# All of w_out loaded ahead of batch 1, whose q, k, v come by halves of heads and are worked off between the output products of chunk 0; kv masked in one op per pair

## Chip, cores, metric

One core of one Trainium2 chip. The metric is device time in microseconds (us) of one execution. The chip and the granted TensorE clock are named where they matter.

Engines: PE is TensorE (PEld its weight loads), ACT ScalarE, DVE VectorE, POOL GpSimd, SP the engine that issues most loads and stores.

## The reference

```python
# q, k, v: (8 batches, 8 heads, 576 rows, 64), float32
q_s = softmax(q, axis=-1)          # per row
k_s = softmax(k, axis=2)           # over the 576 rows
kv  = einsum('bhsd,bhse->bhde', k_s, v)
x   = einsum('bhsd,bhde->bhse', q_s, kv)      # -> (4608, 512)
h   = x @ w_in                     # (512, 2048)
g   = h * sigmoid(beta * h)
out = g @ w_out                    # (2048, 512)
```

## The kernel before

The rows are worked off in nine chunks of 512: chunks 0 to 6 are the first 512 rows of batches 0 to 6, chunk 7 the last 64 rows of all batches, chunk 8 the first 512 rows of batch 7. A chunk has 64 h products (16 units of four, each unit ending in one tanh on ScalarE and one product g on DVE) and 64 output products, all 128x128 by 512 columns. While chunk n runs, batch n+1's attention is prepared between its units ("hooks"). Batches 0 and 1 have nothing to hide behind: batch 0 is worked off at the start, batch 1 between chunk 0 and chunk 1.

```python
    def kv_half(b, half):                  # batches 2 to 7
        kv_mm(b, 2 * half)                 # both halves in bank K
        kv_mm(b, 2 * half + 1)
        kv_norm(b, 2 * half, 2)            # reciprocal, then two ops of 64 rows each

    def h_bank(n, i):
        if n == 0 and i < 12:
            return ("H0", "H1", "H2", "A0", "A1")[i % 5]
        ...
    # loads: q0, k0 (both halves), v0, w_in, w_out 0..11, then
    #        q1, k1, v1, w_out 12..15, q2, k2, v2      (13 buffers)
    ...
        if n == 0:
            b_mm(44)                       # 44 output products of chunk 0
            q_exp(1, 0, 4); q_exp(1, 4, 8) # (one per line in the kernel)
            ...                            # sums, divisions, k_exp
            q_t_pe(1, 0, nc.vector, "X0")
            b_mm(4)
            q_t_pe(1, 1, nc.vector, "H2")
            ...
            lead_in(1, ...)                # v casts, kv, x, with products on
                                           # zeros as fillers
```

The softmax here doesn't subtract the row's maximum and nothing guards it: scores larger than these inputs give would overflow.

Of the kernel before, what the change touches and what calls it, by code (L numbers as in the profile page):

```python
# [16 lines left out]
def kernel(  # L17
# [56 lines left out]
    w_out_b = const.tile([P, NJ, DM], BF16, name="w_out_b")  # L74
    kvp = [const.tile([P, HP, P], BF16, name=f"kvp{b}") for b in range(B)]
# [191 lines left out]
    def v_cast(b, h, eng):  # L267
        hf, a = divmod(h, 4)
        cast(
            eng,  # L270
            va[b % 2][:, 1:K5, h // 2, (h % 2) * D : (h % 2 + 1) * D],
            ld["v", b, hf][:, a, D:].rearrange("p (t d) -> p t d", t=K5 - 1),
        )
# [3 lines left out]
    def kv_mm(b, j, n="K"):  # L277
# [3 lines left out]
        for t in range(K5):  # L281
# [5 lines left out]
            )  # L287

# [21 lines left out]
    def kv_half(b, half):  # L310
        kv_mm(b, 2 * half)
        kv_mm(b, 2 * half + 1)
        kv_norm(b, 2 * half, 2)
# [43 lines left out]
    def h_bank(n, i):  # L357
        if n == 0 and i < 12:
            return ("H0", "H1", "H2", "A0", "A1")[i % 5]
        if n == 1 and i < 2:  # L360
            return ("X0", "H1")[i]
        return f"H{(n * NJ + i) % 3}"
# [26 lines left out]
    for n in range(NCH):  # L389
        if n == 0:  # L390
            bq += [(n, st, j) for j in range(12) for st in range(4)]
            bq += [(n, st, j) for st in (2, 3, 0, 1) for j in range(12, NJ)]
            continue
# [3 lines left out]
        for st in (2, 3):  # L397
# [5 lines left out]
    def b_mm(m):  # L403
        while m and pos[0] < len(bq):
# [3 lines left out]
            if j == 0:  # L408
                name = (f"A{st % 2}", ("A0", "A1", "X1", "K")[st])[n == 0]
                acc[n, st] = bank(name, [P, DM], F32, f"acc{n}_{st}")  # L410
            nc.tensor.matmul(  # L411
                acc[n, st][:],
                gs[n, j][:, st * P : (st + 1) * P],
                w_out_b[:, j, :],
# [8 lines left out]
    def store(n, st):  # L423
        o = osp.tile([P, DM], F32, tag="o", name=f"o{n}_{st}")
        if n == 0 and st % 2:
# [12 lines left out]

    nc.vector.memset(zero[:], 0.0)  # L439
    for hf in range(2):  # L440
        load_q(0, hf)
    for hf in range(2):
        load_kv("k", k, 0, hf, True)
    load_kv("v", v, 0, 0, True)
    load_kv("v", v, 0, 1, True, 0, 2)
    load_kv("v", v, 0, 1, True, 2, 4)
    nc.scalar.activation(beta_h[:, 0:1], zero[:, 0:1], ACTF.Exp)
    nc.scalar.dma_start(beta_r[:], moe_beta.rearrange("(j p) -> j p", p=P))
    load_w_in(0, 256)
# [4 lines left out]
    for j0 in range(0, 12, 2):  # L454
# [8 lines left out]
    nc.vector.tensor_reduce(even[:], evens[:], axis=AX.X, op=ALU.add)  # L463
    for i in range(2):
# [5 lines left out]
    for b in range(B):  # L470
# [11 lines left out]
    q_sum(0, 0, 4)  # L482
    q_sum(0, 4, 8)
    q_div(0, 0, NT, nc.gpsimd, 0, 4)
    q_div(0, 0, NT, nc.vector, 4, 8)
    k_exp(0, 0, 4)
    k_exp(0, 4, 8)
    q_t_pe(0, 0, nc.vector)
    dummy(3)
    q_t_pe(0, 1, nc.vector)  # L490
# [3 lines left out]
    dummy(4)  # L494



    def lead_in(b, kb, xb, fill):
        v_first(b, 0)
        v_cast(b, 0, nc.gpsimd)  # L500
        v_cast(b, 1, nc.gpsimd)
        v_cast(b, 2, nc.scalar)
        v_cast(b, 3, nc.vector)
        fill(0)
        kv_mm(b, 0, kb[0])
        kv_mm(b, 1)
        v_first(b, 1, 0, 1)
        v_cast(b, 4, nc.gpsimd)
        v_cast(b, 5, nc.scalar)
        v_first(b, 1, 1, 2, nc.scalar)  # L510
        v_cast(b, 6, nc.gpsimd)
        v_cast(b, 7, nc.scalar)
        kv_mm(b, 2, kb[1])
        kv_norm(b, 0, 2)
        fill(1)
        x_mm(b, 0, xb[0])
        kv_mm(b, 3)
        x_mm(b, 1, xb[1])
        kv_norm(b, 2, 1)
        x_out(b, 0, nc.scalar)  # L520
        x_out(b, 1, nc.scalar)
        fill(2)
        x_mm(b, 2, xb[2])
        kv_norm(b, 3, 1)
        x_out(b, 2, nc.vector)
        if b == 0:
            cast_w_in(0, 0, nc.gpsimd, 0, 128)
            cast_w_in(0, 0, nc.gpsimd, 128, 256)
        fill(3)
        x_mm(b, 3, xb[3])  # L530
# [132 lines left out]
```

## Time and profile before

| | before |
|---|---|
| time | 294.63 us median (294.43 to 294.85, 4 runs) |
| span of the profiled run | 293.0 us |
| TensorE busy | 97% of the span |
| first h product that is followed without a break | 17.66 us |
| first output product of chunk 0 | 31.62 us |
| first h product of chunk 1 | 49.23 us, after 48 output products |
| last product to end of span | 3.9 us |

How to read a row of the following table of busy time by stretch: the stretch in us, its length, then busy us of PE, PEld, DVE, ACT, POOL (with instruction counts), the granted clock, the DMA share and GB/s.

```profile
0.00:16.40 16.40, 14.72 (x78) 6.52 (x79) 10.31 (x25) 8.75 (x12) 10.82 (x31) 1.00 0.92 306
...
31.60:42.60 11.00, 11.00 (x61) 5.31 (x60) 6.61 (x8) 5.79 (x7) 5.56 (x7) 1.00 1.05 344
42.60:49.20 6.60, 4.45 (x39) 2.32 (x37) 4.25 (x14) 2.51 (x6) 3.16 (x5) 1.00 0.99 329
49.20:80.00 30.80, 30.12 (x154) 14.15 (x154) 21.84 (x43) 21.81 (x38) 8.21 (x13) 1.00 0.80 248
80.00:110.00 30.00, 30.00 (x162) 14.19 (x160) 18.71 (x39) 19.32 (x34) 8.91 (x15) 1.00 0.75 188
...
289.00:293.00 4.00, 0.10 (x1) 0.00 (x0) 0.00 (x0) 0.60 (x1) 0.00 (x0) 1.00 0.17 66
```

From 49 us on TensorE looks full. What can be gained lies in the first 49 us and in the last 4. Each 512-column product is recorded with 0.38 us, while the next one starts 0.216 us later (the Trainium skill, "Trainium Kernel Development and Optimization", Performance Expectations: matmuls are pipelined).

TensorE's timeline around batch 1, and the place where batch 2's kv products wait (start, length, what; in brackets the idle time before it and what ended it):

```profile
41.12 0.61 PE L210 MATMUL tp<-ident,Eq 128*128 128x128 bf16 x8
...
44.31 1.01 PE L282 MATMUL kv<-va,Ek 128*128 128x130 bf16 x15 [0.63 <-DVE va L265]
45.16 0.59 PE L625 MATMUL spare<-zero 128*128 128x512 bf16 x2
...
48.05 0.39 PE L323 MATMUL x<-qT,kvp 128*128 128x512 bf16 x1 [1.02 <-DVE kvp L303]
...
49.23 1.89 PE L368 MATMUL h<-xT,w_in_b 128*128 128x512 bf16 x8 [0.35 <-DVE xT L158]
...
66.79 0.73 PE L282 MATMUL kv<-va,Ek 128*128 128x130 bf16 x10 [0.66 <-DVE kvp L303]
```

The reader is to see a chain of single steps from 41 to 49 us, with products on zeros ("spare") in its gaps, and one visible wait at 66.8 us.

The same later, in batch 4. Its second kv half starts 1.04 us after the four h products ahead of it, although four products take 0.863. No idle time is noted, because the 0.18 us lie under the recorded end of the last h product:

```profile
148.46 1.03 PE L368 MATMUL h<-xT,w_in_b 128*128 128x512 bf16 x4
149.32 0.73 PE L282 MATMUL kv<-va,Ek 128*128 128x130 bf16 x10
...
150.75 1.03 PE L368 MATMUL h<-xT,w_in_b 128*128 128x512 bf16 x4
151.79 0.39 PE L282 MATMUL kv<-va,Ek 128*128 128x130 bf16 x4
```

The end of the span: the last eviction takes 0.60 us and its store follows.

```profile
289.19 0.60 ACT L428 ACTIVATE o<-acc 128x512 f32<-128x512 f32 x1 [2.90 <-PE acc L411]
```

### The profile page before, as it was taken

The page shows a single profiled execution, that of the slowest core. Times are in us where ns is not written, and L with a number is a line of the kernel's source. Part 1 is how long each engine was busy: PE and PEld are TensorE (multiplying, and loading weights), DVE is VectorE, ACT ScalarE, POOL GpSimd, SP SyncE. Part 2 cuts the span into 40 slices and gives each one's busy share as a digit, 9 for nine tenths or more (in the row PEclk, how much of TensorE's full clock was granted, in tenths as well). Part 3 has the DMA queues.
Part 4 walks back from the last instruction along what each step waited for, and adds up shares of the span by engine and source line. Part 5 has one row for each costly group of instructions (what it writes and reads, how often), then busy time and mean ns, then how long its engine had stood idle before and what let it go on. Part 6 is the DMA issues. An engine that isn't in the chain of part 4 may idle for free.

```text
span 293.0 us, 4194 instructions
## 1 busy us (share of the span) xinstructions
PE 283.7 (97%) x1453; PEld 131.7 (45%) x1453; DVE 162.0 (55%) x309; ACT 168.9 (58%) x274; POOL 77.4 (26%) x131
## 2 busy tenths in 40 slices
PE   8999997999999999999999999999999999999994
PEld 3534443444445444544454445444544444444441
DVE  3867385966766466655665576547554433443300
ACT  4566473874884568456855685468544544354411
POOL 8476743450171027101720062106200000000000
PEclk9999999999999999999999999999999999999999
DMA  7999999879459935991399329911410110031111
GB/s 237 357 385 385 362 327 346 295 184 362 100 142 304 284 42 130 313 294 36 105 281 337 50 78 261 360 39 73 107 39 0 72 39 36 0 73 38 36 72 72
DMA packets 54966, 51.67 MB, mean 176 GB/s; under 512 B 21136, under 2 KB 46752, under 8 KB 54944
## 3 DMA queue, kind: packets, MB, share of 16 engines
q1 hardware_dynamic: 54912, 51.39, 58.7%
q8 instruction: 11, 0.18, 0.3%
q14 instruction: 11, 0.09, 0.1%
q10 hardware_dynamic: 32, 0.01, 0.0%
HBM read 38.28 MB, written 9.44 MB: 163 GB/s over the span
## 4 chain that ended last, share of the span: by engine, by line
PE 82%; DMA 14%; DVE 2%; issue 1%; ACT 0%; POOL 0%; SPq 0%; ACTq 0%; POOLq 0%
PE acc L411 39%; PE h L368 37%; DMA v<-in_v_dram 5%; DMA wo<-in_moe_w_out_dram 4%; DMA wi<-in_moe_w_in_dram 3%; PE kv L282 3%; PE x L323 2%; DMA q<-in_q_dram 2%; DVE kvp L303 1%; POOL va L153 0%; PE xt L338 0%; DVE xT L158 0%; ACT th L380 0%; DVE g L382 0%; DVE rk L293 0%
## 5 line engine op out<-in xcount | busy, mean ns | idle before, releaser
L382 DVE SCALAR_TENSOR_TENSOR g<-th,h 128x512 bf16<-128x512 bf16 x144 | 98.6, 686 | 102.5 <-ACT th L380 102.3
L380 ACT ACTIVATE th<-h,beta_h 128x512 bf16<-128x512 f32 x144 | 98.7, 687 | 94.7 <-PE h L368 94.0
L411 PE MATMUL acc<-w_out_b,g 128*128 128x512 bf16 x576 | 145.9, 379 | 0.0
L368 PE MATMUL h<-xT,w_in_b 128*128 128x512 bf16 x512 | 129.2, 379 | 1.2 <-DVE g L382 0.6
L368 PEld LDWEIGHTS <-w_in_b 128*128 128x128 bf16 x576 | 56.3, 98 | 69.5 <-issue 2.2
L411 PEld LDWEIGHTS <-g 128*128 128x128 bf16 x576 | 55.3, 98 | 63.9 <-issue 1.0
L193 POOL TENSOR_TENSOR Eq<-Eq,qz 128x512 bf16<-128x512 bf16 (+1 forms) x26 | 28.9, 1113 | 94.4 <-DVE qz L190 70.5
L428 ACT ACTIVATE o<-acc 128x512 f32<-128x512 f32 x34 | 20.2, 594 | 9.0 <-PE acc L411 9.0
L251 ACT ACTIVATE Ek<-k 128x640 bf16<-128x640 f32 (+1 forms) x28 | 22.6, 806 | 2.7 <-DMA k<-in_k_dram 2.7
L189 DVE TENSOR_REDUCE qz<-Eq 128x8 f32<-128x512 bf16 (+1 forms) x28 | 21.2, 756 | 5.1 <-ACT Eq L181 5.1
L181 ACT ACTIVATE Eq<-q 128x512 bf16<-128x512 f32 (+1 forms) x28 | 19.3, 690 | 6.4 <-DMA q<-in_q_dram 6.4
L153 POOL TENSOR_SCALAR_AFFINE_SELECT va<-v 128x256 bf16<-128x256 f32 x56 | 20.8, 407 | 5.2 <-DMA v<-in_v_dram 4.7
L368 PE MATMUL h<-xTt,w_in_b 128*128 128x512 bf16 x64 | 16.4, 379 | 0.0
L323 PE MATMUL x<-qT,kvp 128*128 128x512 bf16 x32 | 12.2, 381 | 1.6 <-DVE kvp L303 1.5
L282 PE MATMUL kv<-va,Ek 128*128 128x130 bf16 x160 | 11.9, 219 | 1.3 <-DVE kvp L303 0.7
L144 ACT CAST xT<-x 128x512 bf16<-128x512 f32 (+1 forms) x18 | 9.9, 557 | 5.7 <-PE x L323 5.7
L477 PE MATMUL warm<-zero 128*128 128x512 bf16 x37 | 11.8, 471 | 1.3 <-DVE zero L439 1.3
L282 PEld LDWEIGHTS <-Ek 128*128 128x128 bf16 x160 | 10.1, 97 | 6.5 <-issue 4.4
L158 DVE CAST xT<-x 128x512 bf16<-128x512 f32 (+1 forms) x16 | 10.4, 652 | 0.8 <-PE x L323 0.5
L303 DVE TENSOR_TENSOR kvp<-kv,rk 64x128 bf16<-64x128 f32 (+1 forms) x36 | 9.9, 274 | 0.9
L235 POOL TENSOR_TENSOR Et<-Et,zt 128x512 bf16<-128x512 bf16 x4 | 4.2, 1042 | 22.4 <-ACT th L380 11.4
L153 POOL TENSOR_SCALAR_AFFINE_SELECT w_in_b<-wi 128x1024 bf16<-128x1024 f32 (+1 forms) x9 | 8.5, 945 | 4.7 <-DMA wi<-in_moe_w_in_dram 4.7
(44 smaller groups left out, 73.5 us busy)
## 6 DMA issues: line engine op xcount, KB each, us to landing
k<-in_k_dram SPq DMA_DIRECT2D x28, 320.0 KB, 6.5
v<-in_v_dram SPq DMA_DIRECT2D x26, 320.0 KB, 7.6
q<-in_q_dram SPq DMA_DIRECT2D x16, 512.0 KB, 5.2
out_dram<-o SPq DMA_DIRECT2D x32, 256.0 KB, 2.5
wi<-in_moe_w_in_dram SPq DMA_DIRECT2D x8, 512.0 KB, 7.8
wo<-in_moe_w_out_dram SPq DMA_DIRECT2D x8, 512.0 KB, 12.2
k<-in_k_dram SPq DMA_DIRECT2D x4, 256.0 KB, 7.1
qt<-in_q_dram SPq DMA_DIRECT2D x8, 128.0 KB, 7.9
```

Source lines behind the costliest of these rows:

```text
L153: nc.gpsimd.affine_select(out=dst, in_=src, pattern=[[0, n]], base=0, channel_multiplier=0, compare_op=ALU.is_equal, fill=fill0,)
L181: nc.scalar.activation(Eq[b][:, :, h0:h1, :].rearrange("p t h d -> p h t d"), ld["q", b, hf][:, a : a + h1 - h0, :].rearrange("p h (t d) - ...
L189: nc.vector.tensor_reduce(qz[b][:, :, h], Eq[b][:, :, h, :], axis=AX.X, op=ALU.add)
L193: eng.tensor_tensor(Eq[b][:, t0:t1, h0:h1], Eq[b][:, t0:t1, h0:h1], qz[b][:, t0:t1, h0:h1].unsqueeze(3).to_broadcast((P, t1 - t0, h1 - h0, ...
L251: nc.scalar.activation(Ek[b][:, :, h0:h1, :].rearrange("p t h d -> p h t d"), ld["k", b, hf][:, a : a + h1 - h0, :].rearrange("p h (t d) - ...
L282: nc.tensor.matmul(kvs[b, j // 2][:, j % 2, :], Ek[b][:, t, 2 * j : 2 * j + 2, :].rearrange("p h d -> p (h d)"), va[b % 2][:, t, j, :], st ...
L323: nc.tensor.matmul(xps[b, j][:], kvp[b][:, j, :], qT[b][:, :, j, :], start=True, stop=True)
L368: nc.tensor.matmul(hs[n, i][:], w_in_b[:, kt, i * P : (i + 1) * P], rhs_a(n, kt), start=(kt == 0), stop=(kt == KT - 1),)
L380: nc.scalar.activation(th[:], h[:], ACTF.Tanh, scale=beta_h[:, i : i + 1])
L382: nc.vector.scalar_tensor_tensor(out=g[:], in0=th[:], scalar=1.0, in1=h[:], op0=ALU.add, op1=ALU.mult)
L411: nc.tensor.matmul(acc[n, st][:], gs[n, j][:, st * P : (st + 1) * P], w_out_b[:, j, :], start=(j == 0), stop=(j == NJ - 1),)
L428: nc.scalar.activation(o[:], acc[n, st][:], ACTF.Copy, scale=0.5)
```

## The change

Intent: fill TensorE with more of chunk 0's output products while batch 1 lands, and let batch 1's steps follow each other in smaller pieces with output products between them. The parts:

1. Load order: all eight w_out pieces ahead of batch 1; k and v by halves of heads (k half 0, v half 0, k half 1, v half 1); the first w_in piece in two.
2. Batches 0 and 1 are worked off per pair of heads in banks of their own, with one masked op per pair. The 64 output products of chunk 0 are dealt out: 32, exps of q1, 16, exp of k1, 9, then 2, 1, 1, 1 between batch 1's steps, two left for chunk 1.
3. Chunk 0's h products use five banks throughout; the hooks of chunk 1 move back by one or two units.
4. Batches 2 to 7: the second kv half goes to an X bank.
5. The last output tile is computed in two column halves, the second one evicted by two engines and stored in two pieces.

```diff
+    def kv_mask(b, j):
+        ...
+        nc.vector.scalar_tensor_tensor(
+            out=kvp[b][:, j, :], in0=kv1[b, j][:, 0 : 2 * D], scalar=rks[b, j][:, 0:1],
+            in1=mask[:], op0=ALU.mult, op1=ALU.mult,
+        )
     def kv_half(b, half):
-        kv_mm(b, 2 * half)
+        kv_mm(b, 2 * half, xbank() if half else "K")
     def h_bank(n, i):
-        if n == 0 and i < 12:
+        if n == 0:
             return ("H0", "H1", "H2", "A0", "A1")[i % 5]
+    def loads(b):
+        for hf in range(2):
+            load_q(b, hf)
+        load_kv("k", k, b, 0, True)
+        load_kv("v", v, b, 0, True)
+        load_kv("k", k, b, 1, True)
+        load_kv("v", v, b, 1, True, 0, 2)
+        load_kv("v", v, b, 1, True, 2, 4)
-    for j0 in range(0, 12, 2):
+    for j0 in range(0, NJ, 2):
         load_w_out(j0)
+    def batch_1():
+        b_mm(32)
+        q_exp(1, 0, 4)
+        q_exp(1, 4, 8)
+        q_sum(1, 0, 4)
+        q_div(1, 0, NT, nc.gpsimd, 0, 4)
+        b_mm(16)
+        k_exp(1, 0, 4)
+        q_sum(1, 4, 8)
+        q_div(1, 0, NT, nc.vector, 4, 8)
+        b_mm(9)
+        q_t_pe(1, 0, nc.vector, "X0")
+        for h in range(4):
+            v_cast(1, h, nc.scalar if h % 2 else nc.gpsimd, 0)
+        kv_pair(1, 0, "X1")
+        kv_pair(1, 1, "K")
+        kv_mask(1, 0)
+        kv_mask(1, 1)
+        q_t_pe(1, 1, nc.vector, "H2")
+        ...
+        b_mm(2)
+        x_mm(1, 0, "X0")
+        b_mm(1)
+        x_mm(1, 1, "H2")
+        ... (heads 4 to 7 in the same way, then nine h products of chunk 1)
```

More of the change, by code (lines that the diff above doesn't have):

```diff
@@ L74 @@
     w_out_b = const.tile([P, NJ, DM], BF16, name="w_out_b")
+    mask = const.tile([P, P], BF16, name="mask")
     kvp = [const.tile([P, HP, P], BF16, name=f"kvp{b}") for b in range(B)]
@@ L265, in v_first, with v_cast @@
             nc.vector.tensor_scalar(dst, src, even[:, 0:1], None, op0=ALU.mult)
-    def v_cast(b, h, eng):
+    def v_cast(b, h, eng, t0=1, t1=K5):
         hf, a = divmod(h, 4)
@@ L270, in v_cast @@
             eng,
-            va[b % 2][:, 1:K5, h // 2, (h % 2) * D : (h % 2 + 1) * D],
-            ld["v", b, hf][:, a, D:].rearrange("p (t d) -> p t d", t=K5 - 1),
+            va[b % 2][:, t0:t1, h // 2, (h % 2) * D : (h % 2 + 1) * D],
+            ld["v", b, hf][:, a, t0 * D : t1 * D].rearrange("p (t d) -> p t d", d=D),
         )
@@ L287, in kv_mm, with ks_pair, kv_pair @@
             )
+    rks: dict = {}
+    kv1: dict = {}
+    def ks_pair(b, j, n):
+        ps = bank(n, [P, 2], F32, f"ks{b}_{j}")
+        for t in range(K5):
+            nc.tensor.matmul(
+                ps[:],
+                Ek[b][:, t, 2 * j : 2 * j + 2, :].rearrange("p h d -> p (h d)"),
+                va[b % 2][:, t, j, 2 * D : VW],
+                start=(t == 0), stop=(t == K5 - 1),
+            )
+        rks[b, j] = atn.tile([P, 1], F32, tag=f"rk{j}", name=f"rks{b}_{j}")
+        nc.vector.reciprocal(rks[b, j][:], ps[:, 0:1])
+    def kv_pair(b, j, n):
+        w = 2 * D if (b, j) in rks else VW
+        ps = kv1[b, j] = bank(n, [P, VW], F32, f"kv{b}_{j}")
+        for t in range(K5):
+            nc.tensor.matmul(
+                ps[:, 0:w],
+                Ek[b][:, t, 2 * j : 2 * j + 2, :].rearrange("p h d -> p (h d)"),
+                va[b % 2][:, t, j, 0:w],
+                start=(t == 0), stop=(t == K5 - 1),
+            )
+    def kv_mask(b, j):
+        if (b, j) not in rks:
+            rks[b, j] = atn.tile([P, 1], F32, tag=f"rk{j}", name=f"rks{b}_{j}")
+            nc.vector.reciprocal(rks[b, j][:], kv1[b, j][:, 2 * D : 2 * D + 1])
+        nc.vector.scalar_tensor_tensor(
+            out=kvp[b][:, j, :], in0=kv1[b, j][:, 0 : 2 * D], scalar=rks[b, j][:, 0:1],
+            in1=mask[:], op0=ALU.mult, op1=ALU.mult,
+        )
     def kv_norm(b, j, n, eng=None):
@@ L357, in h_bank @@
     def h_bank(n, i):
-        if n == 0 and i < 12:
+        if n == 0:
             return ("H0", "H1", "H2", "A0", "A1")[i % 5]
-        if n == 1 and i < 2:
-            return ("X0", "H1")[i]
-        return f"H{(n * NJ + i) % 3}"
+        if n == 1 and i < 4:
+            return ("H0", "A0", "H1", "H2")[i]
+        return f"H{(n * NJ + i + 1) % 3}"
     def unit_mm(n, i, k0, k1):
@@ L390 @@
         if n == 0:
-            bq += [(n, st, j) for j in range(12) for st in range(4)]
-            bq += [(n, st, j) for st in (2, 3, 0, 1) for j in range(12, NJ)]
+            for j, w in ((0, 4), (4, 4), (8, 8)):
+                for st in range(4):
+                    bq += [(n, st, j + m) for m in range(w)]
             continue
@@ L396 @@
                 bq += [(n, st, j + m) for m in range(4)]
-        for st in (2, 3):
+        for st in (2, 3, 4)[: 2 + (n == NCH - 1)]:
             bq += [(n, st, j) for j in range(NJ)]
@@ L408, in b_mm @@
             if j == 0:
-                name = (f"A{st % 2}", ("A0", "A1", "X1", "K")[st])[n == 0]
+                name = (f"A{st % 2}", ("X1", "K", "A0", "A1", "")[st])[n == 0]
                 acc[n, st] = bank(name, [P, DM], F32, f"acc{n}_{st}")
+            c0, c1 = 0, DM
+            if n == NCH - 1 and st > 2:
+                c0, c1 = (st - 3) * DM // 2, (st - 2) * DM // 2
             nc.tensor.matmul(
-                acc[n, st][:],
-                gs[n, j][:, st * P : (st + 1) * P],
-                w_out_b[:, j, :],
+                acc[n, st][:, c0:c1],
+                gs[n, j][:, min(st, 3) * P : (min(st, 3) + 1) * P],
+                w_out_b[:, j, c0:c1],
                 start=(j == 0),
@@ L424, in store @@
         o = osp.tile([P, DM], F32, tag="o", name=f"o{n}_{st}")
-        if n == 0 and st % 2:
+        if n == NCH - 1 and st > 2:
+            rows = out[(B - 1) * S : (B - 1) * S + CH, :].rearrange("(p t) e -> p t e", t=NT)
+            for i in range(st - 2):
+                w = DM // 2 // (st - 2)
+                c0 = (st - 3) * DM // 2 + i * w
+                if st == 3 or i:
+                    nc.vector.tensor_scalar(
+                        o[:, c0 : c0 + w], acc[n, st][:, c0 : c0 + w], 0.5, None, op0=ALU.mult
+                    )
+                    nc.sync.dma_start(rows[:, 3, c0 : c0 + w], o[:, c0 : c0 + w])
+                else:
+                    o2 = osp.tile([P, DM], F32, tag="o", name=f"o{n}_{st}b")
+                    nc.scalar.activation(
+                        o2[:, 0:w], acc[n, st][:, c0 : c0 + w], ACTF.Copy, scale=0.5
+                    )
+                    nc.scalar.dma_start(rows[:, 3, c0 : c0 + w], o2[:, 0:w])
+            return
+        if n == 0 and st == 3:
             nc.vector.tensor_scalar(o[:], acc[n, st][:], 0.5, None, op0=ALU.mult)
@@ L436, in store @@
             nc.sync.dma_start(rows[:, st, :], o[:])
-    nc.vector.memset(zero[:], 0.0)
-    for hf in range(2):
-        load_q(0, hf)
-    for hf in range(2):
-        load_kv("k", k, 0, hf, True)
-    load_kv("v", v, 0, 0, True)
-    load_kv("v", v, 0, 1, True, 0, 2)
-    load_kv("v", v, 0, 1, True, 2, 4)
+    def loads(b):
[6 more added lines that the diff above has]
+        load_kv("v", v, b, 1, True, 2, 4)
+    nc.vector.memset(zero[:], 0.0)
+    loads(0)
     nc.scalar.activation(beta_h[:, 0:1], zero[:, 0:1], ACTF.Exp)
     nc.scalar.dma_start(beta_r[:], moe_beta.rearrange("(j p) -> j p", p=P))
-    load_w_in(0, 256)
+    load_w_in(0, 256, 0, 2)
+    load_w_in(0, 256, 2, 4)
     load_w_in(256, 512)
@@ L463 @@
     nc.vector.tensor_reduce(even[:], evens[:], axis=AX.X, op=ALU.add)
+    nc.vector.memset(mask[:], 0.0)
+    for h in range(2):
+        nc.vector.memset(mask[h * D : (h + 1) * D, h * D : (h + 1) * D], 1.0)
     for i in range(2):
@@ L469 @@
         )
-    for b in range(B):
+    for b in range(2, B):
         nc.gpsimd.memset(kvp[b][:], 0.0)
@@ L482 @@
     q_sum(0, 0, 4)
+    q_div(0, 0, NT, nc.gpsimd, 0, 4)
     q_sum(0, 4, 8)
-    q_div(0, 0, NT, nc.gpsimd, 0, 4)
+    k_exp(0, 0, 4)
     q_div(0, 0, NT, nc.vector, 4, 8)
-    k_exp(0, 0, 4)
-    k_exp(0, 4, 8)
-    q_t_pe(0, 0, nc.vector)
-    dummy(3)
-    q_t_pe(0, 1, nc.vector)
+    for h in range(4):
+        v_cast(0, h, nc.scalar if h % 2 else nc.gpsimd, 0)
+    ks_pair(0, 0, "A0")
+    ks_pair(0, 1, "A1")
+    q_t_pe(0, 0, nc.vector, "X0")
     bt = bank("H1", [P, NJ], F32, "bt")
@@ L493 @@
     nc.vector.tensor_scalar(beta_h[:], bt[:], 0.5, None, op0=ALU.mult)
-    dummy(4)
-    def lead_in(b, kb, xb, fill):
-        v_first(b, 0)
-        v_cast(b, 0, nc.gpsimd)
-        v_cast(b, 1, nc.gpsimd)
-        v_cast(b, 2, nc.scalar)
-        v_cast(b, 3, nc.vector)
-        fill(0)
-        kv_mm(b, 0, kb[0])
-        kv_mm(b, 1)
-        v_first(b, 1, 0, 1)
-        v_cast(b, 4, nc.gpsimd)
-        v_cast(b, 5, nc.scalar)
-        v_first(b, 1, 1, 2, nc.scalar)
-        v_cast(b, 6, nc.gpsimd)
-        v_cast(b, 7, nc.scalar)
-        kv_mm(b, 2, kb[1])
-        kv_norm(b, 0, 2)
-        fill(1)
-        x_mm(b, 0, xb[0])
-        kv_mm(b, 3)
-        x_mm(b, 1, xb[1])
-        kv_norm(b, 2, 1)
-        x_out(b, 0, nc.scalar)
-        x_out(b, 1, nc.scalar)
-        fill(2)
-        x_mm(b, 2, xb[2])
-        kv_norm(b, 3, 1)
-        x_out(b, 2, nc.vector)
-        if b == 0:
-            cast_w_in(0, 0, nc.gpsimd, 0, 128)
-            cast_w_in(0, 0, nc.gpsimd, 128, 256)
-        fill(3)
-        x_mm(b, 3, xb[3])
-        x_out(b, 3, nc.scalar, 0, 2)
-        x_out(b, 3, nc.vector, 2, 4)
-        for i in range(2 - b):
-            unit_mm(b, i, 0, 3)
@@ L536, in loads_1 @@
-    def loads_1():
-        for hf in range(2):
-            load_q(1, hf)
-        for hf in range(2):
-            load_kv("k", k, 1, hf, True)
-        load_kv("v", v, 1, 0, True)
-        load_kv("v", v, 1, 1, True, 0, 2)
-        load_kv("v", v, 1, 1, True, 2, 4)
-        load_w_out(12)
-        load_w_out(14)
-        for hf in range(2):
-            load_q(2, hf)
-        for hf in range(2):
-            load_kv("k", k, 2, hf)
-            load_kv("v", v, 2, hf)
-    lead_in(0, ("K", "A0"), ("X0", "X1", "A1", "H1"), lambda m: dummy((1, 3, 1, 1)[m]))
+    kv_pair(0, 0, "K")
@@ new lines @@
+    kv_pair(0, 1, "X1")
+    q_t_pe(0, 1, nc.vector, "H0")
+    dummy(2)
+    k_exp(0, 4, 6)
+    k_exp(0, 6, 8)
+    kv_mask(0, 0)
+    kv_mask(0, 1)
+    v_cast(0, 4, nc.gpsimd, 0)
+    v_cast(0, 5, nc.vector, 0)
+    ks_pair(0, 2, "A0")
+    ks_pair(0, 3, "A1")
+    x_mm(0, 0, "X0")
+    kv_pair(0, 2, "K")
+    x_mm(0, 1, "H0")
+    v_cast(0, 6, nc.scalar, 0)
+    v_cast(0, 7, nc.gpsimd, 0)
+    kv_mask(0, 2)
+    x_out(0, 0, nc.scalar)
+    dummy(1)
+    kv_pair(0, 3, "X1")
+    kv_mask(0, 3)
@@ L553 @@
+    x_out(0, 1, nc.vector)
+    for k0 in (0, 2):
+        for m0 in (0, 128):
+            cast_w_in(0, k0, nc.gpsimd, m0, m0 + 128)
+    x_mm(0, 2, "X0")
+    x_out(0, 2, nc.scalar)
+    for i in range(2):
+        unit_mm(0, i, 0, 1)
+    x_mm(0, 3, "K")
+    x_out(0, 3, nc.vector, 0, 2)
+    x_out(0, 3, nc.scalar, 2, 4)
+    LEAD = (2, 3)
+    for k0, k1 in ((1, 2), (2, 3)):
+        for i in range(2):
+            unit_mm(0, i, k0, k1)
     cast_w_in(256, 0, nc.gpsimd)
@@ L555 @@
         for k0 in (0, 2):
-            cast_w_in(n0, k0, nc.gpsimd)
-    for j0 in range(0, 12, 2):
-        cast_w_out(j0, nc.gpsimd)
-        if j0 == 2:
-            loads_1()
+            if n0 == 512 and k0:
+                cast_w_in(n0, k0, nc.gpsimd, 512, 768)
+                cast_w_in(n0, k0, nc.gpsimd, 768, 1024)
+            else:
+                cast_w_in(n0, k0, nc.gpsimd)
+    for j0 in range(0, NJ, 2):
+        cast_w_out(j0, nc.gpsimd)
+        if j0 == 6:
+            loads(1)
+    for hf in range(2):
+        load_q(2, hf)
+    for hf in range(2):
+        load_kv("k", k, 2, hf)
+        load_kv("v", v, 2, hf)
+    def batch_1():
[10 more added lines that the diff above has]
+        q_t_pe(1, 0, nc.vector, "X0")
+        for h in range(4):
+            v_cast(1, h, nc.scalar if h % 2 else nc.gpsimd, 0)
[4 more added lines that the diff above has]
+        q_t_pe(1, 1, nc.vector, "H2")
+        k_exp(1, 4, 6)
+        k_exp(1, 6, 8)
+        v_cast(1, 4, nc.gpsimd, 0)
+        v_cast(1, 5, nc.gpsimd, 0)
+        b_mm(2)
+        x_mm(1, 0, "X0")
+        b_mm(1)
+        x_mm(1, 1, "H2")
+        x_out(1, 0, nc.scalar)
+        b_mm(1)
+        kv_pair(1, 2, "X1")
+        kv_mask(1, 2)
+        v_cast(1, 6, nc.gpsimd, 0)
+        v_cast(1, 7, nc.scalar, 0)
+        x_out(1, 1, nc.scalar)
+        b_mm(1)
+        kv_pair(1, 3, "K")
+        kv_mask(1, 3)
+        x_mm(1, 2, "X0")
+        x_out(1, 2, nc.scalar)
+        for i in range(3):
+            unit_mm(1, i, 0, 1)
+        x_mm(1, 3, "H2")
+        x_out(1, 3, nc.vector, 0, 2)
+        x_out(1, 3, nc.scalar, 2, 4)
+        for i in range(3):
+            unit_mm(1, i, 1, 2)
+        for i in range(3):
+            unit_mm(1, i, 2, 3)
     hooks: dict = {}
@@ L569 @@
         b = n + 1
+        s = 2 if n == 1 else 0
         for m in range(4):
-            at(n, m, lambda b=b, m=m: q_exp(b, 2 * m, 2 * m + 2))
-            at(n, m + 1, lambda b=b, m=m: q_sum(b, 2 * m, 2 * m + 2))
-            at(n, m + 1, lambda b=b, m=m: q_div(b, 0, NT, nc.gpsimd, 2 * m, 2 * m + 2))
-            at(n, 4 + m, lambda b=b, m=m: k_exp(b, 2 * m, 2 * m + 2))
-        at(n, 5, lambda b=b: q_t_dma(b))
+            at(n, s // 2 + m, lambda b=b, m=m: q_exp(b, 2 * m, 2 * m + 2))
+            at(n, s // 2 + m + 1, lambda b=b, m=m: q_sum(b, 2 * m, 2 * m + 2))
+            at(n, s // 2 + m + 1, lambda b=b, m=m: q_div(b, 0, NT, nc.gpsimd, 2 * m, 2 * m + 2))
+            at(n, s + 4 + m, lambda b=b, m=m: k_exp(b, 2 * m, 2 * m + 2))
+        at(n, s // 2 + 5, lambda b=b: q_t_dma(b))
         for h in range(8):
-            at(n, 5 + h // 4, lambda b=b, h=h: v_cast(b, h, nc.gpsimd))
+            at(n, s + 5 + h // 4, lambda b=b, h=h: v_cast(b, h, nc.gpsimd))
         for hf in range(2):
-            at(n, 6 + hf, lambda b=b, hf=hf: v_first(b, hf))
+            at(n, s + 6 + hf, lambda b=b, hf=hf: v_first(b, hf))
         if b + 1 < B:
@@ L585 @@
         s = 1 if n == 1 else 0
-        at(n, 9 + s, lambda b=b: kv_half(b, 0))
-        at(n, 10 + s, lambda b=b: kv_half(b, 1))
+        at(n, 9 + 2 * s, lambda b=b: kv_half(b, 0))
+        at(n, 10 + 2 * s, lambda b=b: kv_half(b, 1))
         for j in range(HP):
@@ L602 @@
         for i in range(NJ):
-            unit_a(n, i, 3 if n < 2 and i < 2 - n else 0)
+            unit_a(n, i, 3 if n < 2 and i < LEAD[n] else 0)
             for f in hooks.get((n, i), []):
@@ L606 @@
             if n:
-                b_mm(0 if n == 1 and i < 1 else 4)
+                b_mm(4)
         if n == 0:
-            b_mm(44)
-            q_exp(1, 0, 4)
-            q_exp(1, 4, 8)
-            q_sum(1, 0, 4)
-            q_sum(1, 4, 8)
-            q_div(1, 0, NT, nc.gpsimd, 0, 4)
-            q_div(1, 0, NT, nc.vector, 4, 8)
-            for hf in range(2):
-                k_exp(1, 4 * hf, 4 * hf + 4)
-            q_t_pe(1, 0, nc.vector, "X0")
-            b_mm(4)
-            q_t_pe(1, 1, nc.vector, "H2")
-            spare = bank("H0", [P, CH], F32, "spare")
-            def idle_1(m):
-                for _ in range((3, 2, 1, 1)[m]):
-                    nc.tensor.matmul(
-                        spare[:], zero[:, 0:P], zero[:], start=True, stop=True
-                    )
-            lead_in(1, ("H1", "X0"), ("H2", "H1", "X0", "H2"), idle_1)
-            cast_w_out(12, nc.gpsimd)
-            cast_w_out(14, nc.gpsimd)
+            batch_1()
     b_mm(10000)
```

## The prediction

> **What bounds the kernel now.** From 49.2 us on it is TensorE: busy time by stretch shows it idle 0.7 us in 49.2 to 80 and 0.0 from there to 289. Four 512-column products take 0.863 us in the chain, 215.8 ns each, the 518 cycles of the Trainium skill ("TensorE: Matmul & The Clock Gate", Back-to-back issue gap); the trace agrees. The DMA engines are full until 40 us; a 512 KB weight piece lands every 1.36 us. So only 0 to 49.2 us, one bank wait and the drain after 289.1 can give anything. At 49.2 us 64 h and 48 output products (24.2 us) and some 6.5 us of attention products are done: about 18 us are lost, 9 of them to the first loads.
>
> **What changes, costed.**
> 1. Start. k0, v0 come by halves, the first w_in piece in two. In the timelines v0's first half landed at 11.7 us; now 10.1. Following the chain by the trace's durations, six h products are done at 16.6 us, not 17.66. Then w_in binds (last cast ends at 27.0 in both). Five banks throughout chunk 0 remove the 0.64 us wait at 28.2. h products end at 30.1, not 31.6.
> 2. w_out ahead of batch 1: two more pieces, so q1, k1, v1 land 2.7 us later, the last at 46.4 instead of 43.6. In return 57 output products (12.3 us), not 44, fill TensorE until 42.4; most of the other seven stand between batch 1's steps.
> 3. Batch 1. Before, 5.6 us passed from the last v1 landing to uninterrupted h products. Now only heads 4 to 7 hang on it: cast 0.5, five kv products 0.3, reciprocal and one masked op 0.45 (was 0.65), x 0.25; nine h products cover the evictions. I expect the last x product at 48.8 us with 62 output and 3 h products done, against 49.2 with 48 and 3: 14 products (3.0 us) plus 0.4, and small change: 3.5 to 4.1 us gained.
> 4. Given back: chunk 1 starts with two output products left, not 16. In its first units DVE needs g 0.6 + row sum 0.65 + reciprocal 0.2, 1.4 us a unit, against 0.86 to 1.1 on TensorE: three waits for H banks, about 1.2 us (0.4 to 2).
> 5. Second kv half in another bank: the 0.66 us wait at 66.8, in batch 2 alone, goes.
> 6. End: last output tile by columns; a 128-column eviction (0.25, was 0.60) and 64 KB (was 256): about 0.5 gained.
>
> Batches 2 to 7 and chunks 2 to 8 keep their products.
>
> **Sum:** -4.1 -0.6 -0.5 +1.2 = about -4. Predicted 290.4 us, 8 in 10 between 288.4 and 292.3. Faster by over 2% (under 288.75): 0.14; within 2%: 0.85; slower: 0.01.
>
> **What would show it.** 1: output products start near 30 us. 2: last v1 cast after 46; output products in one piece to about 42.4, no wait for w_out. 3: chunk 1's h products from 48; TensorE idle in 42 to 48 below 1.5 us. 4: idle of about 1.2 us in 50 to 58, ended by DVE g, DVE near full there. 5: no idle ended by kvp in batch 2. 6: last product to end of span 3.4 us, was 3.9.
>
> **What would make it wrong.** q1's chain (exp, sum, POOL division) ending after 43 us; stores and evictions on ScalarE delaying batch 1's exps; v1 landing after 46.5 because loads wait for buffers; bank waits in chunk 1 above 2 us; or a gain above 6 us because batch 1's loads limit less than I think.

## The result

290.19 us median (289.61 to 290.71, 4 runs) against 294.63. The ratio of the times is 0.9849, 95% interval 0.9827 to 0.9871: 1.5% shorter. A ratio here is the mean time of one kernel's fast runs over that of the other's of the same rounds, so it is not quite the ratio of the medians. The profiled run's span is 288.7 us, 4.3 less than before.

The same stretches after:

```profile
0.00:16.40 16.40, 12.89 (x89) 6.33 (x91) 9.66 (x25) 8.58 (x12) 10.50 (x32) 1.00 0.92 302
...
31.60:42.60 11.00, 10.95 (x52) 4.98 (x52) 4.00 (x6) 3.96 (x5) 7.17 (x10) 1.00 1.08 361
42.60:49.20 6.60, 5.63 (x50) 3.41 (x50) 4.68 (x11) 5.04 (x10) 3.54 (x6) 1.00 1.06 346
49.20:80.00 30.80, 29.88 (x149) 13.73 (x150) 23.73 (x49) 23.70 (x41) 10.34 (x15) 1.00 0.79 248
```

In 42.6 to 49.2 TensorE is busy 5.63 us instead of 4.45, and no longer with fillers; behind that, in 49.2 to 80, it is now less busy (29.88 instead of 30.12). TensorE's timeline after:

```profile
15.97 0.59 PE L405 MATMUL h<-xT,w_in_b 128*128 128x512 bf16 x2 [0.82 <-DVE xT L159]
...
24.19 6.65 PE L405 MATMUL h<-xT,w_in_b 128*128 128x512 bf16 x30 [0.29 <-POOL w_in_b L154]
30.67 12.46 PE L453 MATMUL acc<-w_out_b,g 128*128 128x512 bf16 x56
43.13 0.62 PE L211 MATMUL tp<-ident,Eq 128*128 128x128 bf16 x8
44.52 0.85 PE L310 MATMUL kv<-va,Ek 128*128 128x130 bf16 x10 [0.77 <-POOL va L154]
...
49.06 0.38 PE L360 MATMUL x<-qT,kvp 128*128 128x512 bf16 x1
49.27 1.67 PE L405 MATMUL h<-xT,w_in_b 128*128 128x512 bf16 x7
...
53.64 0.38 PE L453 MATMUL acc<-w_out_b,g 128*128 128x512 bf16 x1
54.25 1.02 PE L405 MATMUL h<-xT,w_in_b 128*128 128x512 bf16 x4 [0.23 <-DVE g L419]
55.11 0.38 PE L453 MATMUL acc<-w_out_b,g 128*128 128x512 bf16 x1
55.64 0.81 PE L405 MATMUL h<-xT,w_in_b 128*128 128x512 bf16 x3
```

The output products run in one piece from 30.67 to 43.1 us (57 in the program; a record is missing). At 49.27 us, 62 output and three h products of chunk 1 are done; before, at 49.23, 48 and none. Those 17 products, 3.67 us, are the gain of the stage, less 0.04.

In 53 to 57 us a new loss shows: an output product at 53.64 should start the next unit at 53.86, but it starts at 54.25. The note says 0.23; from start to start 0.39 are lost. Batch 4's kv halves no longer show the hidden wait (0.87 us from the four h products to the second half instead of 1.04):

```profile
145.28 1.03 PE L405 MATMUL h<-xT,w_in_b 128*128 128x512 bf16 x4
146.14 0.73 PE L283 MATMUL kv<-va,Ek 128*128 128x130 bf16 x10
...
147.57 1.03 PE L405 MATMUL h<-xT,w_in_b 128*128 128x512 bf16 x4
148.44 0.73 PE L283 MATMUL kv<-va,Ek 128*128 128x130 bf16 x10
```

The end: two engines evict 128 columns each, one after the other.

```profile
285.56 0.28 ACT L479 ACTIVATE o_4b<-acc 128x128 f32<-128x128 f32 x1 [2.95 <-PE acc L453]
285.86 0.37 ACTq L482 DMA_DIRECT2D out_dram<-o_4b  x1
285.87 0.29 DVE L473 TENSOR_SCALAR o<-acc 128x128 f32<-128x128 f32 x1 [1.68 <-ACT o_4b L479]
```

### Where the 4.3 us come from

In program order both kernels have done the same 87 output products when chunk 2 begins, and the same work from there on but for the last tile. So the start of each chunk's first tanh on ScalarE, read from its timeline, is a landmark that can be compared (the times in us):

| landmark | before | after | gained so far |
|---|---|---|---|
| chunk 2 | 75.33 | 72.47 | 2.86 |
| chunk 3 | 103.42 | 100.40 | 3.02 |
| chunk 4 | 133.60 | 130.42 | 3.18 |
| chunk 7 | 224.17 | 220.50 | 3.67 |
| last tanh | 277.70 | 274.03 | 3.67 |
| end of span | 293.0 | 288.7 | 4.3 |

From these: the stage up to 49 us 3.63; from there to chunk 2 -0.77 (2.86 less 3.63); chunks 2 to 6 another 0.81 (3.67 less 2.86), 0.16 each; the end 0.63 (4.3 less 3.67). The sum is 4.3. The 0.16 per chunk was in nobody's account: the prediction gave a gain to batch 2 alone and said that the others keep their products.

### The profile page after: what moved, and what is told of

The parts are those of the page before. It is cut to its first block, busy times and chain, and to the rows that moved or that the text cites. A ratio compares the mean times of both kernels' runs of the same rounds, so it can differ in the third digit from the quotient of the medians.

```text
span 288.7 us, 4209 instructions
## 1 busy us (share of the span) xinstructions
PE 278.5 (96%) x1445; PEld 132.8 (46%) x1472; DVE 159.2 (55%) x305; ACT 168.9 (59%) x276; POOL 78.9 (27%) x133
## 4 chain that ended last, share of the span: by engine, by line
PE 80%; DMA 12%; DVE 3%; POOL 2%; ACT 1%; issue 1%; SPq 1%; POOLq 0%; ACTq 0%
PE acc L453 38%; PE h L405 36%; DMA wo<-in_moe_w_out_dram 4%; DMA q<-in_q_dram 4%; PE x L360 2%; DMA k<-in_k_dram 2%; PE kv L283 2%; DMA wi<-in_moe_w_in_dram 2%; DVE g L419 1%; POOL Eq L194 1%; POOL va L154 1%; ACT th L417 0%; SPq L124 0%; DVE qz L190 0%; PE kv L310 0%
## 5 line engine op out<-in xcount | busy, mean ns | idle before, releaser
L453 PE MATMUL acc<-w_out_b,g 128*128 128x512 bf16 (+1 forms) x576 | 143.4, 373 | 1.1
L453 PEld LDWEIGHTS <-g 128*128 128x128 bf16 x592 | 56.9, 98 | 62.5 <-issue 1.2
L154 POOL TENSOR_SCALAR_AFFINE_SELECT va<-v 128x256 bf16<-128x256 f32 (+1 forms) x57 | 22.6, 435 | 3.4 <-DMA v<-in_v_dram 3.4
L159 DVE CAST xT<-x 128x512 bf16<-128x512 f32 (+1 forms) x15 | 9.7, 650 | 1.8 <-PE x L360 1.7
L154 POOL TENSOR_SCALAR_AFFINE_SELECT w_in_b<-wi 128x1024 bf16<-128x1024 f32 (+2 forms) x12 | 8.9, 758 | 3.9 <-DMA wi<-in_moe_w_in_dram 3.8
L543 PE MATMUL warm<-zero 128*128 128x512 bf16 x26 | 8.4, 487 | 1.3 <-DVE zero L507 1.3
L283 PEld LDWEIGHTS <-Ek 128*128 128x128 bf16 x120 | 7.8, 97 | 2.8
L283 PE MATMUL kv<-va,Ek 128*128 128x130 bf16 x120 | 8.8, 220 | 0.0
L154 POOL TENSOR_SCALAR_AFFINE_SELECT w_out_b<-wo 128x1024 bf16<-128x1024 f32 x8 | 8.3, 1041 | 1.6 <-DMA wo<-in_moe_w_out_dram 1.6
```

Source lines behind the costliest of these rows:

```text
L154: nc.gpsimd.affine_select(out=dst, in_=src, pattern=[[0, n]], base=0, channel_multiplier=0, compare_op=ALU.is_equal, fill=fill0,)
L283: nc.tensor.matmul(kvs[b, j // 2][:, j % 2, :], Ek[b][:, t, 2 * j : 2 * j + 2, :].rearrange("p h d -> p (h d)"), va[b % 2][:, t, j, :], st ...
L453: nc.tensor.matmul(acc[n, st][:, c0:c1], gs[n, j][:, min(st, 3) * P : (min(st, 3) + 1) * P], w_out_b[:, j, c0:c1], start=(j == 0), stop=(j ...
```

## Experiments

All timed runs are of five rounds, beside the kernel before on the same chip. The changed kernel was not timed again in them, so a comparison with it, or of e10 to e12 with e5, is one across jobs, through the ratio to the kernel before. Landmarks come from each run's own profile. Part 3 was not run alone: the profile shows only that the wait of 0.64 us at 28.17 us in chunk 0 (for g on DVE) is gone.

### e1_bank_only: part 4 alone

```diff
 # on the kernel before
-        kv_mm(b, 2 * half)
+        kv_mm(b, 2 * half, xbank() if half else "K")
```

> The kernel before with one part of the change alone: the second kv half of a batch goes to an X bank instead of K. Theory A (read from the chunk starts of both traces, 30.17 us apart before and 30.01 after): the half waited for bank K in all six batches of the loop, 0.8 us in batch 2 and about 0.17 us in each of batches 3 to 7, too short to show as idle time. Then the time falls by 1.2 to 1.7 us, to about 293.2, and chunks 3 to 6 start 30.0 us apart. Theory B (the prediction): the wait is in batch 2 alone; then -0.6 us, about 294.0, and the spacing stays 30.17.

Measured: 292.85 us (292.69 to 293.22) against 294.61; ratio 0.9938 (0.9924 to 0.9951). Chunks 3 to 6 start 30.01 to 30.02 us apart; the way from chunk 1 to chunk 2 is 24.23 us instead of 25.05. Theory A holds. By landmarks the bank is worth 1.6 us here: 0.82 in batch 2 and 0.16 in each of the five later batches. (The rest of the measured difference is an earlier chunk 1, by 0.40 us in this profile, of which the edit can have no part.)

### e2_bank_undone: the change without part 4

```diff
 # on the changed kernel
-        kv_mm(b, 2 * half, xbank() if half else "K")
+        kv_mm(b, 2 * half)
```

> The changed kernel with that part undone (both kv halves in bank K). Theory A: 1.2 to 1.7 us longer than the changed kernel, about 291.5, chunks 3 to 6 start 30.17 us apart. Theory B: about 0.6 us longer, 290.8, spacing 30.01.

Measured: 291.10 us (290.71 to 291.51); ratio to before 0.9878 (0.9861 to 0.9895). The spacing is back at 30.17 to 30.18, as theory A says, but the time is only 0.9 us above the changed kernel's, and part of that is a later chunk 1 (51.38 instead of 50.98; see e5). From chunk 1's first tanh to the last one e2 takes 0.66 us longer (223.71 against 223.05). So in the changed kernel the bank is worth about 0.66: 0.81 in batches 3 to 7 (0.16 each), less 0.15 in chunk 1, where batch 2 is prepared. There the kv half waits only 0.17 us without it (65.92 instead of 65.75 us in e2; that the moved hooks are the reason is likely, not shown), and with it an x product waits 0.30 us for the bank that the kv half has taken (67.43 to 67.73 us in the changed kernel). Parts that act on one stage do not add up.

### e3_end_undone: the change without part 5

```diff
 # on the changed kernel
-        for st in (2, 3, 4)[: 2 + (n == NCH - 1)]:
+        for st in (2, 3):
 # and the two special cases for the last tile switched off
```

> The changed kernel with the last output tile as before (one tile of 512 columns, one eviction, one store of 256 KB). If the split ending is what shortens the drain from 3.9 to 3.2 us: 0.6 us longer than the changed kernel, about 290.8, and 3.8 to 3.9 us from the last product to the end of the span. If the drain was set by the receipt of the store alone, no difference above 0.2 us.

Measured: 291.08 us (290.81 to 291.56); ratio to before 0.9874 (0.9856 to 0.9892). From the last tanh to the end of the span 15.22 us, in the changed kernel 14.67: the split end is worth 0.55 us. The rest of the difference of the medians lies at the start, where this profile showed something new:

```profile
8.00:10.00 2.00, 0.37 (x7) 0.12 (x6) 1.93 (x3) 1.27 (x1) 1.30 (x1) 1.00 1.06 360
10.00:12.00 2.00, 2.00 (x35) 1.87 (x34) 1.29 (x5) 1.01 (x3) 0.89 (x2) 0.86 1.09 360
12.00:14.00 2.00, 2.00 (x18) 1.03 (x15) 1.50 (x4) 1.63 (x3) 0.91 (x2) 0.50 1.09 350
```

The column after POOL's is the granted clock. TensorE had run out of products on zeros at 8.25 us and idled 1.63 us; then the clock fell to 0.50, and the first h product came at 16.68 instead of 15.97. The profile of e2 shows the same fall.

### e4_w_out_only: the load order alone, a build with a flaw

```diff
 # on the kernel before: load_w_out(12), (14) moved ahead of batch 1's loads, and
-            b_mm(44)
+            b_mm(60)
             q_exp(1, 0, 4)
```

> The kernel before with only the order of loads changed: all of w_out ahead of batch 1, 60 output products ahead of it instead of 44, batch 1 worked off as before. Theory A: q1, k1, v1 land 2.7 us later, so chunk 1's first h product moves from 49.2 to about 52.0; 16 more output products are done by then (3.45 us), and chunk 1, with none left to fill it, waits about 2 us for H banks behind DVE's row sums. Sum about +1 us: 295 to 296.5. Theory B: the order of w_out is the core of the gain, since it fills TensorE's idle time: 2 to 3.5 us shorter, 291 to 292.6.

Measured: 302.60 us (302.36 to 302.64), 8 us longer than before. Neither theory. The profile's list of waits names the place:

```profile
PE tp L210 <- POOL Eq L193: 5.4, 2, 5.2
```

Sixty output products finish two or three output tiles, and the evictions of finished tiles stand on ScalarE in program order ahead of batch 1's exps. So the exps of q1, landed at 38 us, began at 45.2 us, behind an eviction that waited for TensorE. The edit moved more than the loads; it does not answer its question, but it shows why the change puts the exps between its 32 and its 16 products.

### e9_w_out_only_exps_first: the same, mended

```diff
 # on e4_w_out_only
-            b_mm(60)
+            b_mm(48)
             ... exps, sums, divisions, k exps ...
+            b_mm(12)
             q_t_pe(1, 0, nc.vector, "X0")
```

> e4_w_out_only mended: the exps of batch 1 stand on ScalarE ahead of the evictions of the first finished output tiles, so they no longer wait for TensorE. Theory A (order of loads alone is worth little; the finer batch 1 is the gain): chunk 1's first h product near 52 us instead of 59.4, 16 more output products done, about 2 us lost to H banks in chunk 1: 295 to 296.5, as expected of e4. Theory B: the order of loads alone is the core of the gain: 291 to 292.6.

Measured: 295.80 us (295.70 to 296.09) against 294.53; ratio 1.0045 (1.0031 to 1.0059). Theory A. Chunk 1's first h product is at 52.63 us, 3.4 later, with 16 more output products (3.45 us) done: nothing gained at that point. Then chunk 1, with none left over, waits for g; chunk 2 starts 1.03 us later than before. The load order alone costs about 1.3 us.

### e5_warm29: the changed kernel with a longer warm-up

```diff
 # on the changed kernel
-    dummy(24)
+    dummy(29)
```

> The changed kernel with 29 instead of 24 products on zeros at the start. In two variants of it whose profile was taken, TensorE idled 1.6 us from 8.3 us on and the granted clock then fell to 0.50 between 12 and 14 us; in the changed kernel's own profile it idled 0.9 us and the clock stayed at 1.00. Theory A: that is why the changed kernel's runs spread over 1.1 us where the kernel before spreads over 0.4; then the clock stays at 1.00, first h product near 15.9, and the runs lie at 289.4 to 290.0. Theory B: the spread has another source (the landing of loads): median and spread unchanged within 0.2 us.

Measured: 289.93 us (289.75 to 290.53), ratio to before 0.9849 (0.9836 to 0.9863), the same as the changed kernel's. The clock stays at 1.00 in this profile and in those of e6, e7, e8, e10, e11 and e12, which have the same warm-up. So the dip goes, but the spread does not shrink to what theory A said. What else varies shows over the profiles: the first output product of chunk 0 comes at 31.4 to 31.7 us in four kernels with the old start (before, e1, e4, e9), but at 30.20 in e5, 30.75 in e10, 30.84 in e7, 31.36 in e8 and 31.54 in e11 with the new one. In each of the late ones h products waited for a w_in piece (idle time noted: 0.3 us in e7, 0.5 in e10, 0.9 in e8, 0.7 in e11, none in e5). In all profiles one w_in piece among the later ones lands 0.5 to 1.6 us out of step (GpSimd's idle time ahead of its cast, less the usual 0.31), not always the same one. The old start came late enough to hide that. I did not find its cause.

### e6_delay: does the earlier start count?

```diff
 # on e5_warm29
     def batch_1():
+        late = bank("X0", [P, CH], F32, "late")
+        for _ in range(5):
+            nc.tensor.matmul(late[:], zero[:, 0:P], zero[:], start=True, stop=True)
         b_mm(32)
```

> e5_warm29 with five more products on zeros (1.08 us) ahead of chunk 0's output products. Theory A: the lead of the start is swallowed, since batch 1 waits for its casts of v at 43.6 to 44.5 us whatever TensorE has done by then: 0.1 to 0.4 us longer than e5_warm29. Theory B: TensorE is the limit from the first h product on: 1.0 to 1.1 us longer.

Measured: 291.11 us (290.87 to 292.02), 1.2 above e5_warm29, run on the same chip; ratios to before 0.9892 (0.9877 to 0.9906) and 0.9849. Theory B. In the profiles the output products start 1.43 us later (31.63 and 30.20), and the last tanh is 1.11 later; only 0.35 were swallowed, ahead of the first kv product. My theory that batch 1 waits for v whatever TensorE does is false. The start of the output products, of the kv products and of chunk 1 in e5_warm29 and then in e6_delay:

```profile
30.20 12.47 PE L453 MATMUL acc<-w_out_b,g 128*128 128x512 bf16 x57
43.83 0.85 PE L310 MATMUL kv<-va,Ek 128*128 128x130 bf16 x10 [0.72 <-ACT va L145]
47.72 0.81 PE L405 MATMUL h<-xT,w_in_b 128*128 128x512 bf16 x3
...
31.63 12.46 PE L453 MATMUL acc<-w_out_b,g 128*128 128x512 bf16 x57
44.91 0.82 PE L310 MATMUL kv<-va,Ek 128*128 128x130 bf16 x10 [0.37 <-ACT va L145]
48.82 0.81 PE L405 MATMUL h<-xT,w_in_b 128*128 128x512 bf16 x3
```

### e8_fewer_loads: do batch 1's loads bind?

```diff
 # on e5_warm29; wrong result on purpose
-    for j0 in range(0, NJ, 2):
+    for j0 in range(0, 10, 2):
         load_w_out(j0)
-        cast(eng, w_out_b[:, j0 : j0 + 2, :], ld["wo", j0])
+        cast(eng, w_out_b[:, j0 : j0 + 2, :], ld["wo", min(j0, 8)])
```

> e5_warm29 without the loads of the last three w_out pieces, a wrong result on purpose (the third last piece's data are used for them), so that q1, k1, v1 land 4.1 us earlier. Theory A: the changed kernel is no longer bound by loads in 43 to 49 us but for the gaps between batch 1's steps, about 1.5 us counted from start to start of products: 0.8 to 1.6 us shorter than e5_warm29. Theory B: batch 1 hangs on its loads as before: 3 to 4 us shorter.

Measured: 290.15 us (289.88 to 290.62), ratio 0.9849: not shorter at all. From the first output product to chunk 1's first h product it takes 17.19 us, e5_warm29 17.52, so 0.33 us are saved (an unlucky w_in piece hid that in this profile). The loads did not land 4.1 us earlier, as planned: by the profiles q1 comes 3.0 us earlier than in e5_warm29, v1's first half 2.2 and its last piece 1.4 (44.0 instead of 45.5 us). Counted from the first output product, which is 1.16 us later here, it is 4.2, 3.4 and 2.6 us. The reason stands in ScalarE's timeline:

```profile
42.41 1.26 ACT L252 ACTIVATE Ek<-k 128x1280 bf16<-128x1280 f32 x1
43.64 0.60 ACT L487 ACTIVATE o<-acc 128x512 f32<-128x512 f32 x1
44.14 0.81 ACT L145 CAST va<-v 128x320 bf16<-128x320 f32 x2
```

GpSimd cast its heads of v at 40.5 us, but ScalarE's two casts come in program order behind the eviction of chunk 0's third output tile, which needs the 56th output product (done at about 43.5 us: 31.36 and 56 spacings of 0.216) and stands behind the exp of k. The first kv product follows at 44.64. So once the loads are early TensorE's own speed drives batch 1, through ScalarE's order. In the changed kernel itself the last to be ready is GpSimd's cast of v, which stands behind GpSimd's division (the wait noted at 44.52 us); e8 says that this path and the loads behind it cost no more than 0.33 us.

### e7_k_then_v: are the halves of heads needed?

```diff
 # on e5_warm29, batch 1 only: k half 0, k half 1, v half 0, v half 1
```

> e5_warm29 with batch 1's loads in the old order, both halves of k ahead of v; its last landing stays the same. Theory A (point 3 of the prediction): the first half of the heads must be worked off ahead of the last landing; v's first half lands 1.6 us later, so the first kv product moves from 44.5 to about 45.6 and chunk 1's first h product by as much: 0.8 to 1.2 us longer than e5_warm29. Theory B: only the last landing counts: within 0.2 us.

Measured: 290.54 us (290.34 to 290.88), 0.6 above e5_warm29; ratio to before 0.9868 (0.9854 to 0.9881), intervals that overlap. In the profiles the way from the transposes to the first kv product grows from 1.33 to 1.80 us. That 0.47 is what the order by halves is worth in batch 1; theory A had the direction and twice the size.

### e12_mask_undone: the masked op

```diff
 # on e5_warm29, batches 0 and 1
-        nc.vector.scalar_tensor_tensor(out=kvp[b][:, j, :], ..., in1=mask[:], ...)
+        for h in range(2):
+            r = slice(h * D, (h + 1) * D)
+            nc.vector.tensor_tensor(kvp[b][r, j, h*D:(h+1)*D], kv1[b, j][r, h*D:(h+1)*D],
+                rks[b, j][r, 0:1].to_broadcast((D, D)), ALU.mult)
```

> e5_warm29 with the masked op of batches 0 and 1 undone: two ops of 64 rows each, as before. In the traces the masked op takes 0.35 us and a pair of 64-row ops 0.46, and of the four pairs of batch 1 only those TensorE waits for count. In five traces of the changed kernel's kind the way from batch 1's first kv product to chunk 1's first h product was 3.89 to 3.91 us. Theory A: it grows to 4.0 to 4.2 us and the time by 0.1 to 0.4 us, too little to show against the spread of the runs. Theory B (the op is a main part of the gain): 0.6 us or more.

Measured: 290.88 us (290.83 to 291.26); ratio to before 0.9880 (0.9863 to 0.9896) where e5_warm29 has 0.9849 (0.9836 to 0.9863). About 0.9 us, which favours theory B, with two cautions: the two were run in different jobs, and their intervals touch. (The run also clears kvp of batches 0 and 1 on GpSimd at the start, as before.) The profiles show how 0.1 us per pair grows; chunk 1's first h product comes 1.07 us later in this one. In batch 0 the first h product comes at 16.72 us instead of 15.96. In batch 1 the way from the first kv product to chunk 1's first h product is 4.54 us (44.25 to 48.79) instead of 3.89; of this 0.34 was swallowed ahead of the first kv product, as in e6. Most of it stands here:

```profile
46.94 0.38 PE L364 MATMUL x<-qT,kvp 128*128 128x512 bf16 x1 [0.56 <-DVE qT L159]
```

The second x product waits for bank H2, which holds the transposes of the other half until DVE has copied them, and that copy stands on DVE behind both pairs of masked ops. Each op on DVE delays everything that stands behind it.

### e10_shorter_waits and e11_q_first: attempts at a better version

```diff
 # e10, on e5_warm29
+        q_exp(2, 0, 2); q_sum(2, 0, 2); q_div(...)   # ahead of chunk 1
+        row sums of batch 2 at units 3, 5, 6 instead of 2, 3, 4, 5
+        v casts of batch 1 ahead of the 9 output products
+        second x product of batch 2 in bank K; DVE's eviction of a tile moved to unit 4
+        last tile in parts of 256, 128, 128 columns, each in a bank of its own
 # e11, on e10
+        q1 loaded ahead of w_out 12..15; chunk 0's output products take j 12..15 last
```

> e5_warm29 with four more edits against waits seen in its trace: the row sums of batch 2 spread over chunk 1's first units and one of them moved ahead of it, the casts of v on ScalarE ahead of an eviction, the second x product of batch 2 in bank K, the last two column parts of the last tile in banks of their own. If the waits are what the traces say: start-to-start losses of TensorE in chunk 1 fall from 1.6 us to below 0.6, last product to end of span from 3.2 to about 2.9, the gap ahead of batch 1's first kv product from 0.9 to about 0.6: 1.2 to 1.8 us shorter than e5_warm29, 288.2 to 288.8. If DVE g is not what chunk 1 waits for: 0.3 to 0.6 us.

> e10_shorter_waits with q1 loaded ahead of the last two w_out pieces (chunk 0's output products take j 12 to 15 last), so that batch 1's division and transposes are over before its v lands and DVE and GpSimd no longer work side by side at 43 us. Expected: chunk 1's first h product about 0.8 us earlier; 0.5 to 1.0 us shorter than e10, 287.4 to 288.2. If w_out's last piece now comes too late for the output products: no gain, and a gap in them at 41 us.

Measured: e10 289.80 us (289.08 to 290.84), ratio to before 0.9842 (0.9823 to 0.9861); e11 289.66 us (289.35 to 290.73), ratio 0.9841 (0.9825 to 0.9857). Neither is told apart from the changed kernel. By landmarks e10 saves 0.23 us in chunk 1 (21.25 instead of 21.48) and 0.23 at the end (14.44 instead of 14.67, since the last two evictions no longer share a bank), a third of what I expected. Thinning the row sums moved the waits for g more than it removed them: the next unit still starts at 54.02 with 0.50 us idle noted, and x waits 0.20 for the transpose of q, which now comes later. In e11's profile the output products have a gap of about 0.3 us (their end at 44.13 is 12.59 us after their start, 57 products take 12.30).

## Why the prediction was right

The time was forecast at 290.4 us and measured at 290.19; direction and size were right. Several of its reasons were not, and that their errors cancelled is luck: up to chunk 2 the forecast was 3.5 us (4.1 less 1.2, and 0.6 for the bank) and 2.86 were measured; the 0.81 us of batches 3 to 7, which it did not foresee, made up for it.

1. **Start** (1.5 us earlier output products forecast, 0.95 measured). "Six h products are done at 16.6 us" failed: the first h product waits 0.82 us for bank H0, which holds the second x product of batch 0 until DVE has evicted it. I had followed the data but not the banks. But that is not what the 0.55 us are lost by: e5_warm29 has the same wait for H0, no late w_in piece, and its output products start at 30.20 us, close to the forecast 30.1. The late w_in piece of the changed kernel's profile (24.19 us) accounts for most of the shortfall.
2. **w_out ahead** (right as a description). The output products ran in one piece, to 43.1 us instead of 42.4, with no wait for w_out, and the last v1 casts came after 46 us. But the implied gain does not belong to this step: alone it costs 1.3 us (e9).
3. **Batch 1** (3.5 to 4.1 us forecast, 3.63 measured). The size was right and the reason wrong. I said that heads 4 to 7 "hang on" the last landing. Loads that landed 2.6 to 4.2 us earlier, counted from the first output product, saved 0.33 us (e8), and delaying TensorE by 1.08 us cost about as much (e6). What bounds the stage is the order of work on the helper engines behind TensorE's own products: ScalarE's by e8, DVE's by e12. I also had the count wrong, with three h products done at 49.2 us in the kernel before; there were none, so 17 and not 14 products were gained.
4. **Given back** (1.2 us forecast for H banks). The profile shows 1.26 from start to start, in four waits at 53 to 57 us, each ended within 0.1 us of a g on DVE, plus 0.30 for an X bank that I had not seen. e10 shows that thinning DVE's row sums there recovers only 0.23 us, so how much of it the sums cause is not settled.
5. **Bank of the second kv half.** "In batch 2 alone" was wrong: in the kernel before the wait was in all six batches, 0.8 us and then 0.16 each, together 1.6 us (e1). In the changed kernel the bank is worth 0.66 us (e2), so the forecast of 0.6 was close, but for the wrong batches: the gain is in batches 3 to 7. It was missed because I read idle time instead of start-to-start time.
6. **End** (0.5 forecast, 0.63 in the profiles, 0.55 by e3). Right.

The masked op, which I costed at 0.2 us on one step, is worth about 0.9 us by e12's times. It is part of points 1 and 3, not an addition to them.

Left open: what makes one w_in piece land late, and how much of the spread of the changed kernel (289.61 to 290.71) is due to it and how much to the clock at the start. Also open is how the 3.63 us divide among the rest of part 2: no run has the finer batch 1 without the new order of w_out, so that it is the core of the gain is concluded from e9 (the order alone loses), e7 (0.47 for the halves) and e12, not measured by itself.

## What to carry to other kernels

Read a pipelined engine from start to start: compare the spacing of equal stages in both kernels, because waits shorter than the recorded tail of an instruction show nowhere as idle. Before blaming loads for a stage, make the loads early by force, check in the trace how much earlier they land, and look whether the stage moves; here program order on a helper engine, an eviction ahead of a cast, was the limit. Work taken from the next stage to fill a gap leaves that stage with its own waits: here 1.26 us in the changed kernel and about 1.0 in e9.

## What the Trainium skill lacked or had wrong

- "TensorE: Matmul & The Clock Gate", Part 1 and the table of why it matters, give about 3.4 us of idle for the clock to fall to half and advise against gaps over some 3 us. Here the clock fell after 1.63 us of idle, followed by small products: 0.86 in 10 to 12 us and 0.50 in 12 to 14 (e3_end_undone). With 0.91 us (the changed kernel) and 0.98 us (e7_k_then_v) it stayed at 1.00. This does not contradict the page: from the last product on zeros to the fall it was about 3.2 us (an estimate from the mean clock of 0.72 in 11 to 12 us), and whether the small products in between count as activity no run here decides.
- "TensorE: Matmul & The Clock Gate", Back-to-back issue gap, agrees for 512 columns (215.8 ns by its formula in cycles, 0.863 us for four in the chain). The page's other figure there, about 131 ns per product of 512 columns as a sustained rate in a real kernel, appears in no profile of this case.
- "PSUM — Partial Sum Buffer", PSUM bank collisions, says that two engines must not touch one bank at a time, and that a dependency is put between them. The trace agrees: in the end of the changed kernel DVE starts 0.03 us after ScalarE has finished its part of the same bank. The page lacks the price: splitting one x tile between two engines takes 0.42 and then 0.37 us, where ScalarE alone takes 0.58.
- "SBUF — State Buffer", Who interferes with whom, says that a DVE op with two SBUF inputs contends with GpSimd's reads. The trace agrees and gives a size: two casts on GpSimd took 1.84 us beside DVE's division, and 0.86 almost alone in e8_fewer_loads. DVE's division is lengthened by GpSimd's own division just before these casts: it took 1.59, 1.93 and 2.08 us in the kernel before, the changed one and e8, where the two divisions overlap by 0.51, 0.85 and 0.99 us, so 1.08 us and the whole overlap.
- No page that I used says that a wait shorter than the recorded tail of a product shows as no idle time; here up to 0.16 us each (0.379 recorded, 0.216 spacing).
